# Letting the late weight blocks of a fused attention and two-MoE kernel into decoding in steps, tied to the stores of the second pass

## The chip, the cores and the metric

The kernel runs on one core of a Trainium2 chip. The metric is the device time of one execution in microseconds (us). The kernel before took 993.44 us (median of three executions, 986.15 to 995.56).

## The reference

Attention with a learned decay feeds a dense layer with a clipped gate, and that feeds a layer with the largest of three projections. Sizes: 4 batches, 8 heads, 576 positions, head width 64; 2304 tokens of width 512; inner widths 2048 and 768. The reference works in the precision of its weights, which come as 64-bit numbers.

```python
scores = q @ k.T / 8 + minimum(-(cum[:, None] - cum[None, :]), 0)   # causal, cum = cumsum(max(s, 0))
x  = softmax(scores) @ v                    # -> 2304 x 512
h  = x @ w_in                               # 512 x 2048
x2 = (h * clip(h + 3, 0, 6) / 6) @ w_out    # 2048 x 512
h2 = maximum(maximum(x2 @ w1, x2 @ w2), x2 @ w3)   # 512 x 768, three times
out = h2 @ w_out2                           # 768 x 512
```

## The kernel before

**A planner writes the order.** The kernel is written as coroutines ("threads"). A planner (class `Flow`, from L108) runs them against a small cost model of the engines (`mm`, `dve1`, `act2` and so on, from L196), and each time that it gives an engine to a thread, the thread emits the instruction. So the planner fixes, once and for all, the order of instructions on each engine and on the DMA queue (all DMAs are issued from SP, in `copy`, L306). On the chip each engine runs its list in that order, and waits only for the data and the buffers that an instruction really needs. A thread has a rank: of the threads ready for an engine, the lowest rank goes first. Buffers are held in stocks (`Stock`), and a thread that asks an empty stock waits by rank. A thread can also wait for an `Event`; such a wait exists in the plan only. A DMA's landing is planned by a formula (L184): 0.65 us, plus bytes over 360,000 per us, plus 0.9 us.

**Numbers as pairs.** Matrix products run in a reduced format; every operand is split into a high and a low part, and a product is three matmuls (L429 to L431, helper `three`), accumulated in one PSUM bank.

**Decoding a weight block** (`bits_in`, L373, and `decode`, L412). A block is 128 x 512 numbers of 64 bits, 512 KB. It is loaded into one of two `raw` buffers (stock RAW), squared on ACT (L385), and put together by four DVE instructions (L387, L393, L398, L403); the last frees the raw buffer. `decode` then rounds the block to its high part (L333, on DVE) and subtracts for the low part (L346, on POOL). For the third layer `raw_half` runs `bits_in` alone, straight into one half of a pair tile `wr`; two blocks make a pair, and there are nine pairs (NP2 = 9) for the eighteen blocks of w1, w2 and w3. `out_weight` decodes one of the six blocks of w_out2 (NJ = 6) and stores the result to DRAM (`o2_d`, shown as `o_d`), to be loaded again much later.

**Stages.** In the first (to some 372 us) attention runs, and in its gaps a first pass of the first layer: six of its sixteen inner blocks for all eight token blocks of 288 tokens (u = 0 to 7). Then follows the second pass with the other ten blocks. For each u, `hidden1` (L930) multiplies x by a block of w_in into a bank `ps_h`; `gate` (L951) makes `u` on ACT (L955), `g` on DVE (L959, which also frees the bank), and the pair `gt` (L331 on ACT, L346 on POOL or DVE). `reduce1` (L972) multiplies `gt` by a block of w_out into four banks `ps_x`. When a token block is complete, `x2_out` (L1025) adds, for each of the four banks, the first pass's part (`xf`, L1030 on DVE, which frees the bank), and stores the result to DRAM (`x2_d`, shown as `x_d<-xf`). When the four stores of u have landed, the event `x2_stored[u]` is set. TensorE's list alternates ps_h and ps_x matmuls all through this stage, with ps_h ahead by as many as nine `gt` tiles.

**The third layer** works on two token blocks at a time in seven products instead of eight. For this, `forms` (L1095) and `form` (L1110) make sums and differences of the pair tiles and split them (tiles `ws`, `wf`, `wg`). A form takes three or four buffers of the stock W2. These come from the second pass's weights, as its last token block gives them back, and three of them from `spare_weights` (L1078), which waits until all six blocks of w_out2 are stored. `hidden2` then multiplies (`ps_j`), and `reduce2` does the last product (`ps_o`).

**Ranks around the change.** NS = 160, NB = 10. Decoding of the second pass's weights has ranks 160 to 177, that of the pair blocks 180 to 197, that of w_out2 198 to 203. On engines other than TensorE, `gate` has rank 140 and `x2_out` has rank 200 (`RANKS`).

**Where the late decoding starts.** `main` (L1384) waits for the end of attention and then starts the threads of all forty-four blocks at once, at L1400 to L1409: ten of w_in, ten of w_out, nine pairs, six blocks of w_out2. As only two raw buffers exist, the blocks go through in order of rank.

Of the kernel before, what the change touches and what calls it, by code (L numbers as in the profile page):

```python
# [26 lines left out]
NJ = DF2 // P  # L27
# [227 lines left out]
def attn_moe_moe2(ctx, tc, q, k, v, s, w_in, w_out, w1, w2, w3, w_out2, out):  # L255
# [3 lines left out]
    flow = Flow()  # L259
    NB = NF - NA  # L260

    def event():
        return Event(flow)
# [28 lines left out]
    half = const.tile([P, 1], F32, name="half")  # L292
# [3 lines left out]
    def make(item, shape, dtype, name):  # L296
        pl, tag = item
        if pl is None:
            return views[tag]
        return pl.tile(shape, dtype, tag=tag, name=name, bufs=1)  # L300

    def stack(pl, tag, n):
        return [(pl, f"{tag}{x}") for x in range(n)]
# [66 lines left out]
    def weight(key):  # L370
        return ready.setdefault(key, event())

    def bits_in(src, out):  # L373
        r = yield RAW.get()
        raw = make(r, [P, 512], I64, "raw")
        yield DMA
        copy(raw, src)
        yield flow.landing(8 * P * 512)
        am = yield AM.get()
        m = make(am[1], [P, 512], F32, "dm")  # L380
        a = make(am[0], [P, 512], U32, "da") if out is None else out.bitcast(U32)
        bits = raw.bitcast(U32).rearrange("p (n t) -> p n t", t=2)
        lo, hi = bits[:, :, 0], bits[:, :, 1]
        yield "ACT", act1(512)
        act.activation(m, hi.bitcast(F32), AF.Square)  # L385
        yield "DVE", dve2(512)
        vec.scalar_tensor_tensor(  # L387
            out=m, in0=m, scalar=LEAST * LEAST, in1=hi.bitcast(F32),
            op0=ALU.is_ge, op1=ALU.mult,
        )  # L390
        top = m.bitcast(U32)
        yield "DVE", dve1(512)
        vec.tensor_scalar(  # L393
            out=a, in0=top, scalar1=3, scalar2=0x3FFFFFF8,
            op0=ALU.logical_shift_left, op1=ALU.bitwise_and,
        )
        yield "DVE", dve2(512)
        vec.scalar_tensor_tensor(  # L398
            out=a, in0=top, scalar=0xC0000000, in1=a,
            op0=ALU.bitwise_and, op1=ALU.bitwise_or,  # L400
        )
        yield "DVE", dve2(512)
        vec.scalar_tensor_tensor(  # L403
            out=a, in0=lo, scalar=29, in1=a,
            op0=ALU.logical_shift_right, op1=ALU.bitwise_or,
        )
        RAW.put(r)
        if out is not None:
            AM.put(am)
        return a.bitcast(F32), am  # L410

    def decode(src, store, key):  # L412
        item = yield store.get()
        wf, am = yield from bits_in(src, None)
        dst = make(item, [P, 2, 512], F32R, "w")
        yield from rounded(dst[:, 0, :], wf, 512, ON["wh"])
        yield from minus(dst[:, 1, :], wf, dst[:, 0, :].bitcast(F32), 512, ON["wl"])
        AM.put(am)
        weight(key).set((dst, item))
# [14 lines left out]
    NS = len(seq)  # L434
# [145 lines left out]
    def load(dst, src, nbytes):  # L580
        yield DMA
        copy(dst, src)
        return flow.landing(nbytes)
# [326 lines left out]
    x2_stored = [event() for u in range(NU)]  # L910
# [135 lines left out]
    NP2 = len(PAIRS)  # L1046
# [12 lines left out]
    def raw_pair(n):  # L1059
        item = yield W.get()  # L1060
        r = make(item, [P, 2, 512], F32, "wr")
        raw_item[n].set((r, item))

    def raw_half(n, half):
        r, _ = yield raw_item[n]
        i, j = PAIRS[n][half]
        yield from bits_in((w1, w2, w3)[i][j], r[:, half])
        raw_ready[n][half].set()

    def out_weight(j):  # L1070
        yield from decode(w_out2[j], W, ("o2", j))
        w, item = weight(("o2", j)).value
        ev = yield from load(o2_d[j], w, 8 * P * 512)
        yield ev
        W.put(item)
        o2_stored[j].set()

    def spare_weights():  # L1078
        for j in range(NJ):
            yield o2_stored[j]  # L1080
        for _ in range(2 * NA - NP2):
            W2.put((yield W.get()))
# [12 lines left out]
    def forms():  # L1095
        for n in range(NP2):
            for half in range(2):
                yield raw_ready[n][half]
            r, ri = raw_item[n].value
            items = []  # L1100
            for _ in range(3):
                items.append((yield W2.get()))
            made = [make(item, [P, 2, 2, HK], F32R, "wf") for item in items]
            if n % 2 == 0:
                spare = yield W2.get()
                single = make(spare, [P, 2, 2, HK], F32R, "wg")
            forms_of[n] = items + ([spare] if n % 2 else [])
            flow.start(flow.cur.prio, form(n, r, ri, made, single))
# [271 lines left out]
    def fill(stock_, items):  # L1380
        for item in items:
            stock_.put(item)

    def main():  # L1384
        yield attention_done
        pa.close()
        w2pool = ctx.enter_context(
            tc.tile_pool(name="w2pool", bufs=1, side="right", reuse_waits="tile")
        )
        psb = ctx.enter_context(  # L1390
            tc.tile_pool(name="psb", bufs=1, space=PSUM, side="right", reuse_waits="tile")
        )
        px2 = ctx.enter_context(
            tc.tile_pool(name="px2", bufs=1, side="right", reuse_waits="tile")
        )
        fill(M, stack(psb, "b", 5))
        fill(W2, stack(w2pool, "w", 2 * NB))
        for n in STAGE:
            fill(STAGE[n], [(px2, "xr" + n)])
        for f in range(NB):  # L1400
            flow.start(NS + f, decode(w_in[NA + f], W2, ("i", NA + f)))
        for f in range(NB):
            flow.start(NS + AFTER + f, decode(w_out[NA + f], W2, ("o", NA + f)))
        for n in range(NP2):
            flow.start(NS + 2 * NB + 2 * n, raw_pair(n))
            for half in range(2):
                flow.start(NS + 2 * NB + 2 * n + half, raw_half(n, half))
        for j in range(NJ):
            flow.start(NS + 2 * NB + 2 * NP2 + j, out_weight(j))  # L1409
        flow.start(0, spare_weights())  # L1410
        flow.start(NS, forms())
        yield part_stored[NU - 1]
        fill(XF, stack(mp, "part", 2))
        fill(PT, [(px2, "t0"), (px2, "t1")])
        yield x_over
        p_mx.close()
        mb1 = ctx.enter_context(
            tc.tile_pool(name="mb1", bufs=1, side="right", reuse_waits="tile")
        )
        fill(XFS, stack(mb1, "xf", 8))  # L1420
        for st in (UU, GG):
            XF.put((yield st.get()))
            PT.put((yield st.get()))

        def halved(item, *sts):
            t = make(item, [P, 2, U1], F32, "mm")
            for x, st in enumerate(sts):
                views[item[1], x] = t[:, x]
                st.put((None, (item[1], x)))

        for sts in ((MF, MF), (TMP, TMP), (MF, TMP)):
            halved((yield GT.get()), *sts)
        for _ in range(NG - 3):
            XFS.put((yield GT.get()))
        for j in range(NJ):
            yield o2_stored[j]
        yield mp_over
        for st in (MF, TMP, MF, MF):
            st.put((yield XF.get()))
            (MF if st is MF else TMP).put((yield PT.get()))  # L1440
        for _ in range(2):
            yield RAW.get()
            yield AM.get()
        p_dec.close()
        mb3 = p_out.enter_context(tc.tile_pool(name="mb3", bufs=1, reuse_waits="tile"))
        fill(AM, [((mb3, f"ws{x}"), None) for x in range(2)])
        fill(XFS, stack(mb3, "xf", 4))
        fill(W2, [(mb3, "w")])

    def late_weights():  # L1450
        yield heads[WO_AFTER].ready
        for f in range(NA):
            flow.start(WO_PRIO + WO_STEP * f, decode(w_out[f], W, ("o", f)))
# [15 lines left out]
    flow.start((NS + 2 + RANKS[3], -1), hidden2())  # L1469
    flow.start((NS + 1, -2), reduce2())  # L1470
    flow.start(0, main())
    flow.run()

# [55 lines left out]
```

## Time and profile before

| | |
|---|---|
| median of three executions | 993.44 us (986.15 to 995.56) |
| the profiled execution | 995.07 us |
| its span, first to last instruction | 993.3 us |
| mean granted TensorE clock, as a share of full speed | 0.958 |

The profile is of one execution. It gives each instruction's start and length, and for each idle time of an engine what ended it. A matmul's length overlaps its neighbours', so a stretch's number of matmuls tells its pace better than its busy time. The granted clock is TensorE's, 1.00 being 2.4 GHz; it has two levels, 2.4 and 1.2 GHz, and a share between them is a mean over a stretch.

### The profile page before, as it was taken

To read this page: it belongs to the slowest core of one execution; us is meant where nothing else is said; L and a number is where in the kernel's file an instruction comes from. 1 tells how busy PE (TensorE), PEld (TensorE's weight loads), DVE (VectorE), ACT (ScalarE), POOL (GpSimd) and SP (SyncE) were. 2 spreads that over 40 slices of the span, in tenths; PEclk is the share of its full clock that TensorE was granted. 3 is DMA by queue.
4 is the path that set the end of the run, shared out by engine and by line. 5 is a ranking of instruction groups with operands and counts; after the bars stand their busy time and mean duration, and the time that the engine had idled before them with its cause. 6 is when DMAs were issued, how large, how long until landed. Compare 5 with 4: busy or idle time off the path is not lost.

```text
span 993.3 us, 19077 instructions
## 1 busy us (share of the span) xinstructions
PE 938.8 (95%) x6532; PEld 876.1 (88%) x6532; DVE 693.2 (70%) x1818; ACT 452.4 (46%) x1146; POOL 389.0 (39%) x431
## 2 busy tenths in 40 slices
PE   9998799899899999899899999999799999999998
PEld 5454589889788999799899999999799999999998
DVE  5887889789888728999888842239977676666300
ACT  3566578677676744343443333335433232333311
POOL 4668757656555423444234332225740101021000
PEclk7779799999998999999999999999899999999999
DMA  5789877686684435555676743201203030264522
GB/s 170 188 206 239 234 181 209 174 242 172 171 225 109 144 109 192 177 185 172 182 219 203 249 144 96 85 12 48 84 31 91 25 96 25 67 206 137 162 84 73
DMA packets 87482, 144.56 MB, mean 146 GB/s; under 512 B 9532, under 2 KB 58684, under 8 KB 87384
## 3 DMA queue, kind: packets, MB, share of 16 engines
q1 hardware_dynamic: 87384, 143.33, 49.8%
q8 instruction: 52, 0.85, 0.4%
q14 instruction: 46, 0.38, 0.1%
HBM read 82.79 MB, written 33.96 MB: 118 GB/s over the span
## 4 chain that ended last, share of the span: by engine, by line
PE 60%; DVE 15%; DMA 13%; issue 5%; ACT 3%; SPq 2%; POOL 1%; DVEq 0%; ACTq 0%; POOLq 0%
PE ps_j L430 7%; PE ps_j L431 6%; PE ps_j L429 6%; PE ps_s L762 5%; DMA kt<-kb 5%; PE ps_h L429 3%; PE ps_h L430 3%; PE ps_h L431 3%; PE pt L826 3%; PE ps_x L429 3%; PE ps_x L431 3%; PE ps_x L430 3%; PE px L867 3%; DMA raw<-in_w_dram 3%; PE ps_o L430 3%
## 5 line engine op out<-in xcount | busy, mean ns | idle before, releaser
L429 PE MATMUL ps_x<-gt,w 128*128 128x288 f32 x512 | 155.1, 303 | 7.1 <-DVE g L959 6.7
L346 POOL TENSOR_TENSOR gt<-g,gt 128x288 fp32r<-128x288 f32 x101 | 88.1, 872 | 186.0 <-ACT gt L331 174.4
L429 PE MATMUL ps_h<-x,w 128*128 128x288 f32 x512 | 154.4, 301 | 2.7 <-DVE g L959 1.7
L431 PE MATMUL ps_x<-gt,w 128*128 128x288 f32 x512 | 152.8, 298 | 1.5 <-POOL w L346 1.5
L430 PE MATMUL ps_h<-x,w 128*128 128x288 f32 x512 | 152.0, 297 | 0.0
L430 PE MATMUL ps_x<-gt,w 128*128 128x288 f32 x512 | 151.9, 297 | 0.0
L431 PE MATMUL ps_h<-x,w 128*128 128x288 f32 x512 | 151.7, 296 | 0.0
L340 POOL TENSOR_SCALAR e<-e,tiny 128x256 f32<-128x256 f32 (+4 forms) x152 | 104.8, 696 | 93.8 <-DVE tiny L791 44.4
L430 PE MATMUL ps_j<-xf,wf 128*128 128x288 f32 x432 | 130.0, 301 | 3.1 <-POOL xf L346 2.7
L429 PE MATMUL ps_j<-xf,wf 128*128 128x288 f32 x432 | 129.5, 300 | 2.1 <-DVE xf L333 2.0
L431 PE MATMUL ps_j<-xf,wf 128*128 128x288 f32 x432 | 129.5, 300 | 0.0
L762 PE MATMUL ps_s<-kt,qt 66*128 66x256 f32 (+11 forms) x384 | 102.9, 364 | 14.1 <-DMA kt<-kb 10.4
L785 ACT ACTIVATE e<-e,tiny 64x576 f32<-64x576 f32 (+4 forms) x160 | 95.8, 599 | 38.6 <-DVE tiny L777 33.0
L331 ACT ACTIVATE gt<-g 128x288 fp32r<-128x288 f32 x128 | 56.5, 443 | 119.1 <-DVE g L959 118.9
L959 DVE SCALAR_TENSOR_TENSOR g<-u,ps_h 128x288 f32<-128x288 f32 x128 | 57.1, 446 | 71.6 <-ACT u L955 71.3
L429 PEld LDWEIGHTS ps_x<-gt,w 128*128 128x128 f32 x512 | 97.8, 191 | 9.9 <-DVE g L959 8.1
L429 PEld LDWEIGHTS ps_h<-x,w 128*128 128x128 f32 x512 | 97.1, 190 | 4.1 <-DVE g L959 2.2
L431 PEld LDWEIGHTS ps_x<-gt,w 128*128 128x128 f32 x512 | 97.7, 191 | 1.9 <-POOL w L346 1.9
L430 PEld LDWEIGHTS ps_x<-gt,w 128*128 128x128 f32 x512 | 98.0, 191 | 0.0
L430 PEld LDWEIGHTS ps_h<-x,w 128*128 128x128 f32 x512 | 97.2, 190 | 0.1
L431 PEld LDWEIGHTS ps_h<-x,w 128*128 128x128 f32 x512 | 97.1, 190 | 0.0
L777 DVE CUSTOM_DVE_ANT_0 e<-ps_s,above 64x288 f32<-64x288 f32 (+4 forms) x160 | 75.3, 474 | 30.4 <-PE ps_s L762 29.1
(149 smaller groups left out, 2234.9 us busy)
## 6 DMA issues: line engine op xcount, KB each, us to landing
x<-x_d SPq DMA_DIRECT2D x64, 288.0 KB
kt<-kb SPq DMA_DIRECT2D x90, 144.0 KB
raw<-in_w_out_dram SPq DMA_DIRECT2D x22, 512.0 KB
x_d<-xs SPq DMA_DIRECT2D x16, 576.0 KB
raw<-in_w_dram SPq DMA_DIRECT2D x18, 512.0 KB
qt<-qb SPq DMA_DIRECT2D x30, 288.0 KB
raw<-in_w_in_dram SPq DMA_DIRECT2D x16, 512.0 KB
mh<-m_d SPq DMA_DIRECT2D x48, 144.0 KB
```

Source lines behind the costliest of these rows:

```text
L331: act.activation(dst, src, AF.Copy)
L340: (pool if e == "POOL" else vec).tensor_scalar(out=y, in0=y, scalar1=r, scalar2=1.0, op0=ALU.mult, op1=ALU.mult)
L346: (pool if e == "POOL" else vec).tensor_tensor(out=dst, in0=a, in1=b_, op=ALU.subtract)
L429: pe.matmul(ps, lhsT=wh, rhs=xh, start=first, stop=False, skip_group_check=again)
L430: pe.matmul(ps, lhsT=wh, rhs=xl, start=False, stop=False, skip_group_check=again)
L431: pe.matmul(ps, lhsT=wl, rhs=xh, start=False, stop=last, skip_group_check=again)
L762: pe.matmul(o, lhsT=lhs[:, qs], rhs=rhs[:, lo:hi], start=(x == 0), stop=(x == len(passes) - 1),)
L777: vec.tensor_tensor_reduce(out=e[:n, lo:hi], in0=ps[:n, 0:hi - lo], in1=above[:n, shift + lo:shift + hi], scale=-0.125, scalar=m0, op0=ALU ...
L785: act.activation(e[:n, :w], e[:n, :w], AF.Exp, bias=m0, scale=-1.0, accum_out=r,)
L826: pe.transpose(pt[:, y, :], cut, ident[:n, :n])
L867: pe.matmul(px[:, z:n], lhsT=vhl[:, x, j].rearrange("p l d -> p (l d)"), rhs=src[:, hl, x, z:n], start=(x + hl == 0), stop=(last and hl == 1),
L959: vec.scalar_tensor_tensor(out=g, in0=ut, scalar=1.0, in1=ps, op0=ALU.min, op1=ALU.mult)
```

## The change

The loops that start the pair blocks and the blocks of w_out2 leave `main`. A new thread, `later_weights`, starts them in steps. Pairs 0 and 1 are started when `x2_stored[0]` is set, pairs 2 and 3 at `x2_stored[1]`, 4 and 5 at `x2_stored[2]`, 6 and 7 at `x2_stored[3]`, and pair 8 at `x2_stored[4]`. With pairs 3 to 8 goes one block of w_out2 each. So the five steps hold 4, 5, 6, 6 and 3 blocks. The ranks stay as they were.

```diff
@@ -1401,12 +1401,7 @@
             flow.start(NS + f, decode(w_in[NA + f], W2, ("i", NA + f)))
         for f in range(NB):
             flow.start(NS + AFTER + f, decode(w_out[NA + f], W2, ("o", NA + f)))
-        for n in range(NP2):
-            flow.start(NS + 2 * NB + 2 * n, raw_pair(n))
-            for half in range(2):
-                flow.start(NS + 2 * NB + 2 * n + half, raw_half(n, half))
-        for j in range(NJ):
-            flow.start(NS + 2 * NB + 2 * NP2 + j, out_weight(j))
+        flow.start(0, later_weights())
         flow.start(0, spare_weights())
         flow.start(NS, forms())
         yield part_stored[NU - 1]
@@ -1446,6 +1441,16 @@
         fill(AM, [((mb3, f"ws{x}"), None) for x in range(2)])
         fill(XFS, stack(mb3, "xf", 4))
         fill(W2, [(mb3, "w")])
+
+    def later_weights():
+        for n in range(NP2):
+            if n % 2 == 0:
+                yield x2_stored[n // 2]
+            flow.start(NS + 2 * NB + 2 * n, raw_pair(n))
+            for half in range(2):
+                flow.start(NS + 2 * NB + 2 * n + half, raw_half(n, half))
+            if n > 2:
+                flow.start(NS + 2 * NB + 2 * NP2 + n - 3, out_weight(n - 3))
 
     def late_weights():
         yield heads[WO_AFTER].ready
```

## Rows read from the trace of the kernel before

**Rows 1.** The page's first part: busy time, share of the span, instructions.

```profile
PE 938.8 (95%) x6532; PEld 876.1 (88%) x6532; DVE 693.2 (70%) x1818; ACT 452.4 (46%) x1146; POOL 389.0 (39%) x431
```

**Rows 2.** By stretch: PE, PEld, DVE, ACT, POOL busy; granted clock, DMA share, GB/s.

```profile
372.00:465.00 93.00, 87.79 (x647) 86.86 (x646) 87.92 (x127) 37.31 (x82) 41.29 (x33) 0.98 0.57 177
...
472.00:484.00 12.00, 9.28 (x52) 8.18 (x51) 10.47 (x21) 4.75 (x10) 2.70 (x3) 0.86 0.59 190
484.00:544.00 60.00, 60.00 (x456) 60.00 (x455) 48.77 (x82) 24.80 (x50) 20.88 (x20) 1.00 0.68 210
544.00:552.00 8.00, 6.83 (x48) 6.16 (x48) 5.97 (x12) 2.64 (x6) 2.65 (x3) 1.00 0.69 208
...
576.00:584.00 8.00, 7.27 (x52) 6.66 (x51) 5.05 (x11) 1.67 (x4) 2.86 (x3) 1.00 0.58 201
584.00:640.00 56.00, 56.00 (x426) 56.00 (x425) 11.28 (x25) 17.28 (x37) 15.33 (x19) 1.00 0.25 75
...
675.00:735.00 60.00, 52.81 (x354) 51.45 (x354) 56.90 (x108) 26.48 (x69) 40.09 (x43) 0.91 0.19 56
```

**Rows 3.** TensorE's waits from 465 to 500 us: total, times, longest.

```profile
PE ps_x L431 <- POOL w L346: 1.5, 2, 0.9
PE ps_x L429 <- DVE g L959: 1.2, 1, 1.2
```

**Rows 4.** Timeline of TensorE, 475 to 484 us.

```profile
476.90 0.40 PE L429 MATMUL ps_x<-gt,w 128*128 128x288 f32 x1 [1.21 <-DVE g L959]
...
480.13 0.40 PE L429 MATMUL ps_h<-x,w 128*128 128x288 f32 x1 [1.14 <-DVE g L959]
...
481.25 0.44 PE L430 MATMUL ps_x<-gt,w 128*128 128x288 f32 x1
...
483.64 0.44 PE L431 MATMUL ps_h<-x,w 128*128 128x288 f32 x1
```

**Rows 5.** Timeline of DVE, 470 to 477 us.

```profile
470.43 1.62 DVE L387 SCALAR_TENSOR_TENSOR dm<-dm,raw 128x512 f32<-128x512 f32 x1
...
474.13 0.45 DVE L959 SCALAR_TENSOR_TENSOR g<-u,ps_h 128x288 f32<-128x288 f32 x1
475.65 0.83 DVE L387 SCALAR_TENSOR_TENSOR dm<-dm,raw 128x512 f32<-128x512 f32 x1 [1.07 <-ACT dm L385]
476.41 0.44 DVE L959 SCALAR_TENSOR_TENSOR g<-u,ps_h 128x288 f32<-128x288 f32 x1
```

**Rows 6.** Timeline of the DMA queue on SP, 465 to 614 us.

```profile
465.35 0.33 SPq L306 DMA_DIRECT2D raw<-in_w_dram  x1
...
478.31 0.33 SPq L306 DMA_DIRECT2D x_d<-xf  x1
...
484.76 0.32 SPq L306 DMA_DIRECT2D x_d<-xf  x1
...
570.04 0.34 SPq L306 DMA_DIRECT2D raw<-in_w_out_dram  x1
...
612.70 0.32 SPq L306 DMA_DIRECT2D x_d<-xf  x1
```

**Rows 7.** DVE's groups by line, 465 to 582 us: busy, mean ns, idle before.

```profile
L387 DVE SCALAR_TENSOR_TENSOR dm<-dm,raw 128x512 f32<-128x512 f32 x25 | 18.8, 752 | 13.7 <-ACT dm L385 13.6
...
L403 DVE SCALAR_TENSOR_TENSOR wr<-raw,wr 128x512 uint32<-128x512 uint32 x18 | 15.1, 841 | 0.2
L398 DVE SCALAR_TENSOR_TENSOR wr<-dm,wr 128x512 uint32<-128x512 uint32 x18 | 13.3, 736 | 0.5
L393 DVE TENSOR_SCALAR wr<-dm 128x512 uint32<-128x512 uint32 x18 | 10.2, 569 | 0.2
...
L333 DVE CAST w<-da 128x512 fp32r<-128x512 f32 x8 | 3.8, 472 | 0.1
```

**Rows 8.** DVE's groups by line, 584 to 640 us.

```profile
L959 DVE SCALAR_TENSOR_TENSOR g<-u,ps_h 128x288 f32<-128x288 f32 x19 | 8.6, 454 | 40.2 <-ACT u L955 40.2
```

**Rows 9.** Timeline of DVE: the first instruction of the first form.

```profile
660.71 0.42 DVE L1090 TENSOR_TENSOR ws<-wr 128x256 f32<-128x256 f32 x1
```

## The prediction

> **What bounds the kernel now.** Start with the page's first part: TensorE is busy for 95% of the span, VectorE (DVE) for 70% [rows 1]. So no edit off TensorE can give more than TensorE loses now, and the question is where it loses. Next comes the table by stretch, read by matmul counts, since lengths overlap. In 484 to 544 us TensorE starts 456 matmuls in 60 us, one each 0.1316 us, at a granted clock of 1.00; 584 to 640 has the same pace (426 in 56) [rows 2]. That is the full pace of this stage. Against it:
>
> - 472 to 484: 52 matmuls are worth 6.84 us, so 5.16 us of 12 are lost.
> - 544 to 552: 48 are worth 6.32 us, 1.68 lost.
> - 576 to 584: 52 are worth 6.84 us, 1.16 lost.
> - 675 to 735: 354 are worth 46.6 us, 13.4 lost, with DVE busy for 56.90 of 60 us. This is the forms' stretch, and the changed threads don't run there [all rows 2].
>
> The first three lie where a token block of the second pass ends: its stores stand in the DMA queue from 478.31 to 484.76 for u = 0, and each later token block comes some 32 us after ((612.70 - 484.76) / 4 for u = 0 to 4) [rows 6]. The pair blocks enter the queue at 465.35, and the last block of w_out2 at 570.04 [rows 6], so the changed threads' work lies over all three losses. Then the waits: around the largest one TensorE waits for `g` on DVE, and, before that, for the last block of w_out on POOL (1.5 us) [rows 3]. The timeline shows how: TensorE stands at 476.90 and 480.13 for `g` [rows 4]. On DVE, a decode instruction from 470.43 takes 1.62 us, others follow up to the `g` of 474.13, and the next `g` comes at 476.41, behind a decode instruction that itself sat 1.07 us until ACT had squared a block [rows 5]. DVE works through its list in order, so a `g` that is ready stands behind a decode instruction that isn't.
>
> **The change, part by part.** *What is removed and added:* nothing. The same 24 blocks are loaded, squared, put together and stored. No wait is added on the chip either: the waits for `x2_stored` exist in the plan, and what changes is where the 24 loads, 24 squarings, the DVE work and six stores stand in the lists of SP, ACT, DVE and POOL. The first load behind a store needs only a free raw buffer.
>
> *Size of what is moved.* From the first load to the last, 23 intervals take 104.7 us, 4.55 us a block [rows 6]. On DVE a block costs 0.75 + 0.57 + 0.74 + 0.84 = 2.90 us, with 0.47 more for the rounding of w_out2 [rows 7]; idle before the first of these, for ACT, was 13.6 us over 25 blocks, 0.54 us each [rows 7].
>
> *Where it goes.* The five steps hold 4, 5, 6, 6 and 3 blocks and begin after the stores of u = 0 to 4. I add 2 us for the landing as the planner counts it (0.65 + 0.41 + 0.9). They then last 18.2, 22.8, 27.3, 27.3 and 13.7 us. From the last store of one token block to the first store of the next there are 32 - (484.76 - 478.31) = 25.5 us [rows 6]. So step 0 ends 5 us ahead of the next boundary; step 1 (24.8 us) just reaches it; steps 2 and 3 (29.3 us) run over it; step 4 ends at 612.7 + 15.7 = 628.4, where no boundary is near.
>
> *Boundary of u = 0 (472 to 484).* It loses all its decode work. What stays there on DVE is `g`, `xf` and some `gt`; a boundary without decode work, that of u = 4 inside 584 to 640, loses nothing [rows 2]. The ends are 0 (the wait is owed to the backlog of the earlier decoding, where DVE was busy for 87.92 of 93 us [rows 2]) and -5.2 us. I take -5.2, since the rows on DVE name the decode instructions.
>
> Of the 5.2 us some belong to a slow clock: from 481.25 to 483.64 eleven matmuls start 0.239 us apart [rows 4], nearly twice 0.1316, so the clock was at 1.2 GHz, after the waits of TensorE just told; the stretch's mean is 0.86 [rows 2].
>
> The Trainium skill, "TensorE: Matmul & The Clock Gate", section on HAM oscillation, says that gaps in TensorE's work drop it back to half rate, so that a wait is paid a second time behind it. By this rule, with which the trace agrees here (0.239 us after the waits), the slow stretch goes with the waits, and the sum stands; were it to come anyway, 13 matmuls from 480.84 on by 0.107 us, 1.4 us of the gain would stay lost.
>
> *Boundary of u = 1 (510 to 518).* No loss now, with decode work beside it (inside 484 to 544 [rows 2]), none after: 0.
>
> *Boundary of u = 2 (544 to 552).* Step 1 may or may not be over. Ends 0 and -1.7 us; I take half, -0.8.
>
> *Boundary of u = 3 (576 to 584).* Step 2 lies over it as w_out2 does now. Ends -1.2 and +0.5 (it loses what u = 2 loses now); I take 0.
>
> *Boundary of u = 4 (608 to 613).* Now free; step 3 will lie over it. Ends 0 and +5.2 (what u = 0 loses now); I take +1.4, the mean of the losses now at u = 2 and u = 3, as these are the boundaries whose DVE lists look alike.
>
> *Inside the token blocks.* TensorE loses nothing from 484 to 544 with DVE busy for 48.77 of 60 us [rows 2]. Between 584 and 640 DVE has 11.28 us of work in 56 [rows 2], a `g` every 3 us or so and 40.2 us idle beside them [rows 8]. Steps 3 and 4 bring nine blocks, some 28 us there. That is covered: 0. If that cover were missing, it would show as at u = 4.
>
> *The late end.* The first form starts at 660.71 [rows 9]. `spare_weights` now ends at about 630 (628.4 and a store) instead of some 585, so 30 us of slack hide the delay.
>
> *Sum.* -5.2 + 0 - 0.8 + 0 + 1.4 + 0 = -4.6 us, from -8.1 (the low ends) to +5.7 (the high ends). The profiled execution took 995.07 us, 1.6 above the median of 993.44. 995.07 - 4.6 = 990.5 for such an execution; by the median, **988.8 us**.
>
> **Rivals.**
>
> *A, the stall doesn't come from the decoding.* DVE comes out of 372 to 465 with a backlog (95% busy) and TensorE first waits for the last w_out block on POOL [rows 2, 3]; `g` would be late in any case. Against it: the instructions ahead of the late `g` are decode instructions of the moved blocks [rows 5]. Gain 0: 993.4 us.
>
> *B, the stall moves with the decoding (the slower side).* A step starts as a burst, two loads at once with an empty ring, and ends about when the next token block does. `x2_out` has rank 200 and the decoding 180 to 203, so at a boundary the plan lets decode instructions go ahead of nearly every `xf`, and banks stay taken. Place: boundaries of u = 2, 3 and 4. Price: each pays what u = 0 pays now, so -5.2 + (5.2 - 1.7) + (5.2 - 1.2) + 5.2 = +7.5: 1000.9 us. It decides from the point where a block takes more than 25.5 / 6 = 4.2 us in steps 2 and 3, and where TensorE has no `gt` in stock. For it: 4.55 us a block. Against: u = 2 and 3 have such work now and pay 1.7 and 1.2.
>
> *C, the whole loss goes.* With pauses between the steps DVE catches up, and all three boundaries run at full pace: -5.2 - 1.7 - 1.2 = -8.1: 985.4 us. For it: at u = 1 decode work costs nothing now. Against: steps 2 and 3 leave no pause.
>
> *D, the forms wait.* If the last block of w_out2 is stored after 660.71 instead of near 630, W2 lacks three buffers and each us past it is lost; ten late would give 1003 us. Against: 30 us of slack [rows 6, 9].
>
> *E, the change does not do what it says.* If TensorE and its feeders run behind the plan, loads planned after a store may run beside the next boundary all the same; by its result that is A (993.4 us) or B (1000.9 us), and its chance is counted in theirs.
>
> **How the numbers follow.** The forecast gets 0.48, A 0.20, C 0.15, B 0.12, D 0.05. The forecast's own range goes from 985 (C's end) to 993 (A's end). The three executions of before lie 9.4 us apart, so medians move by some 4 us on their own. Downward I go 5 us below C, to 980; upward to 1000, which takes in A whole and about half of B. Left out are half of B, D, and a small tail of C: under 2 in 10. About 1%, 9.9 us, is what a measurement of this kernel can tell from no change. Faster by more than that (under 983.5) needs C with a good draw, or the forecast with a very good one: 0.15 x 0.4 + 0.48 x 0.15 = 0.13, and 0.01 from A: 0.14. Slower by more (over 1003.4): D's 0.05 halved and a third of B: 0.07. The rest, 0.79, is within 1%.
>
> **What would show it.** Right: no raw load in the queue between the last block of w_out and the last store of u = 0; some 90 matmuls in the 12 us around that boundary at a granted clock of 1.00; a raw load shortly behind each of the stores of u = 0 to 4; the last store of w_out2 near 625; DVE busy for 35 to 45 us from 584 to 640, instead of 11.28, with TensorE still at 0.1316 us a matmul; the first form within a few us of 655. Wrong: waits for `g` at the first boundary without decode work ahead of them (A); new waits for `g` or `xf` near 608, 579 or 545 with a granted clock below 1.00 behind them (B); a first form held by its buffers (D). A shift of more than some us within the forms' stretch would lie outside all of these.

## The result, and the profile after

The changed kernel is faster: 981.71 us (median of thirteen executions, 978.68 to 985.40) against 991.38 us (thirteen executions, 986.15 to 995.56). The ratio is 0.9917, with a 95% interval from 0.9899 to 0.9936, so 8.2 us are gained, between 6.3 and 10.0 (the medians alone lie 9.7 us apart). The forecast was 4.6 us, to 988.8 us.

The profiled execution of the changed kernel took 978.72 us, with a span of 976.9 us. Its span is 16.4 us shorter than that of the kernel before [the page's head], twice what the timing shows, and so the first thing to do is to split this difference. The lists of TensorE, DVE, ACT and POOL are the same in both kernels up to the last block of w_out; TensorE's is the same to its end. The subtraction for the low part of that block (`w<-da,w` on POOL, the last one ahead of the stores of u = 0) is a mark that both traces have. In the timeline of POOL of the kernel before (start, length, engine, line):

```profile
470.23 1.28 POOL L346 TENSOR_TENSOR w<-da,w 128x512 fp32r<-128x512 f32 x1 [1.82 <-DVE w L333]
```

and of the changed kernel:

```profile
462.00 1.28 POOL L346 TENSOR_TENSOR w<-da,w 128x512 fp32r<-128x512 f32 x1 [1.82 <-DVE w L333]
```

The changed kernel's execution is 8.23 us ahead there, before the first instruction on DVE, ACT or POOL that the change moved. In the kernel before the first late load is in the queue by then (465.35 [rows 6]), but it has no part in this: matched matmul by matmul, TensorE is 8.2 us ahead already at 350 us, in the attention stage. That half is the difference between two executions of the same lists, not the change. From the end of attention on executions of the same lists agree better: from the matmul that the kernel before starts at 372 us to the mark, the nine traces with the same lists there took between 98.2 and 98.9 us. From here on every time is counted from this mark.

In the DMA queue of the changed kernel:

```profile
470.25 0.32 SPq L306 DMA_DIRECT2D x_d<-xf  x1
...
471.14 11.31 SPq L306 DMA_DIRECT2D raw<-in_w_dram  x4
...
613.16 0.33 SPq L306 DMA_DIRECT2D o_d<-w  x1
...
629.89 0.32 SPq L306 DMA_DIRECT2D x_d<-xf  x1
...
696.57 0.33 SPq L306 DMA_DIRECT2D x_d<-xf  x1
```

and two later stores in that of the kernel before:

```profile
644.69 0.32 SPq L306 DMA_DIRECT2D x_d<-xf  x1
...
711.22 0.33 SPq L306 DMA_DIRECT2D x_d<-xf  x1
```

The reader is to see two things. The late loads now stand behind the last store of u = 0 (470.25, then 471.14), where before they stood ahead of the first [rows 6], and the last store of w_out2 comes at 613. And the gain can be followed along the marks:

| from the mark to | before | changed | difference |
|---|---|---|---|
| last store of u = 0 | 14.53 us | 8.25 us | -6.3 us |
| last store of u = 5 | 174.46 us | 167.89 us | -6.6 us |
| last store of u = 7 | 240.99 us | 234.57 us | -6.4 us |
| end of the span | 523.1 us | 514.9 us | -8.2 us |

Most of the gain is there after the first boundary. A last 1.8 us come in the forms' stretch and behind. The stores between these marks say less, as a store also shifts with the DVE work around it (last store of u = 4: 142.5 and 139.7 us). TensorE's 6532 matmuls, matched one by one, split the 8.2 us behind the mark better: 5.4 us are gained at the boundary of u = 0, 1.3 at that of u = 2, nothing in the end at u = 3, 0.3 are lost at u = 4, and 1.7 are gained in the forms' stretch. The table by stretch of the changed kernel (columns as in [rows 2]); the first row lies to the mark as 472 to 484 did, the next three run from the last store of one token block to that of the next (u = 2, 3 and 4), the last is the forms' stretch, moved by the 14.7 us that it starts earlier:

```profile
463.77:475.77 12.00, 12.00 (x93) 12.00 (x92) 4.02 (x10) 5.14 (x12) 4.03 (x5) 1.00 0.60 185
500.67:535.74 35.07, 34.77 (x263) 34.51 (x262) 24.38 (x39) 11.98 (x25) 13.30 (x12) 1.00 0.60 195
535.74:569.40 33.66, 32.72 (x246) 32.25 (x245) 25.62 (x43) 13.21 (x28) 12.52 (x12) 1.00 0.61 197
569.40:601.73 32.33, 32.33 (x245) 32.09 (x244) 23.41 (x41) 12.60 (x26) 9.41 (x10) 1.00 0.64 200
...
660.30:720.30 60.00, 53.51 (x371) 52.15 (x370) 57.76 (x106) 26.88 (x70) 40.63 (x44) 0.94 0.19 56
```

TensorE has 93 matmuls where it had 52 (the view counts those that reach over an edge), at a granted clock of 1.00 instead of 0.86, and DVE is busy for 4.02 us instead of 10.47. At 0.1316 us a matmul 41 more are 5.4 us. At u = 2 now 35.07 - 263 x 0.1316 = 0.46 us are lost (1.68 before), at u = 3 1.29 (1.16 before), at u = 4 0.09 (none before). In DVE's timeline the boundary of u = 0 looks like this:

```profile
463.52 0.44 DVE L959 SCALAR_TENSOR_TENSOR g<-u,ps_h 128x288 f32<-128x288 f32 x1
464.86 0.45 DVE L959 SCALAR_TENSOR_TENSOR g<-u,ps_h 128x288 f32<-128x288 f32 x1 [0.90 <-ACT u L955]
465.23 0.81 DVE L1030 TENSOR_TENSOR xf<-ps_x,pt 128x288 f32<-128x288 f32 x2
...
475.85 0.69 DVE L387 SCALAR_TENSOR_TENSOR dm<-dm,raw 128x512 f32<-128x512 f32 x1 [0.25 <-ACT dm L385]
```

Each `g` and `xf` starts as its data comes, and the first decode instruction of the late blocks comes more than 13 us behind the mark; before, it came 0.2 us behind it [rows 5].

### The profile page after: what moved, and what is told of

It is laid out like the page before. It is cut to its first block, busy times and chain, and to the rows that moved or that the text cites. A ratio compares the mean times of both kernels' runs of the same rounds, so it can differ in the third digit from the quotient of the medians.

```text
span 976.9 us, 19063 instructions
## 1 busy us (share of the span) xinstructions
PE 931.7 (95%) x6532; PEld 870.5 (89%) x6532; DVE 701.5 (72%) x1819; ACT 451.7 (46%) x1146; POOL 390.0 (40%) x430
## 4 chain that ended last, share of the span: by engine, by line
PE 66%; DVE 14%; DMA 9%; issue 5%; POOL 2%; ACT 2%; SPq 2%; DVEq 0%; POOLq 0%; ACTq 0%
PE ps_j L430 6%; PE ps_j L431 6%; PE ps_j L429 6%; PE ps_s L762 6%; PE ps_x L429 4%; PE ps_h L429 4%; PE ps_h L430 4%; PE ps_x L431 4%; PE ps_h L431 4%; PE ps_x L430 4%; PE pt L826 3%; DMA kt<-kb 3%; PE px L867 3%; PE ps_o L430 3%; PE ps_o L431 3%
## 5 line engine op out<-in xcount | busy, mean ns | idle before, releaser
L955 ACT ACTIVATE u<-ps_h,half 128x288 f32<-128x288 f32 x128 | 63.5, 496 | 61.2 <-PE ps_h L431 60.6
```

Of the source, the lines that this page charges most:

```text
L955: act.activation(ut, ps, AF.Relu, bias=half, scale=1.0 / 6.0)
```

## The experiments

TensorE's own list is the same in the kernel before, the changed kernel and all experiments but the last two: only the lists of DVE, ACT, POOL and SP differ. The ratios come from three sets, each against the kernel before on one chip: the first four experiments; the two with landings 2 us later together with the two that only move the rounding; the remaining four. A ratio of one set is compared with that of another, or with the changed kernel's 0.9917, across sets. At the end of this section one table has those with the same list.

**All late blocks together, behind the stores of u = 0.** The pauses go, the free boundary stays.

```diff
     def later_weights():
         for n in range(NP2):
-            if n % 2 == 0:
-                yield x2_stored[n // 2]
+            if n == 0:
+                yield x2_stored[0]
```

> All 24 late blocks start together when the stores of token block u = 0 have landed; no steps after that. Theory T (the loss sits at the boundary of u = 0, where DVE comes out of the backlog of the w_out decoding, and only the absence of decode work there counts): the gain stays nearly whole, 6 to 8 us, ratio 0.992 to 0.994 to the kernel before; TensorE starts some 90 matmuls in the 12 us around the boundary of u = 0. Theory P (the pauses between the steps are what counts): at most 3 us, 0.997 or more, with new losses at u = 1 to u = 3.

Measured: 0.9944 (0.9919 to 0.9968), 5.5 us. The 12 us at the boundary of u = 0, in the table by stretch:

```profile
463.64:475.64 12.00, 12.00 (x93) 12.00 (x92) 4.02 (x10) 5.03 (x11) 4.04 (x5) 1.00 0.60 184
```

93 matmuls, as in the changed kernel. So theory T holds, a hair above its range: one free boundary is worth most of the gain. Whether the four further steps add the remaining 2.7 us can't be said, as the intervals of 0.9917 and 0.9944 overlap.

**The first step at once, the others as changed.**

```diff
-            if n % 2 == 0:
+            if n % 2 == 0 and n > 0:
                 yield x2_stored[n // 2]
```

> Pairs 0 and 1 start at the end of attention as before, so they follow the last w_out block at once; pairs 2 to 8 and w_out2 keep the steps of the changed kernel. Theory T: four blocks last some 18 us and cover the boundary of u = 0 as before, so the loss of 5 to 6 us there comes back; ratio 0.998 to 1.000. Theory P: most of the gain stays, ratio 0.993 to 0.995.

Measured: 0.9987 (0.9961 to 1.0012). The same 12 us, and TensorE's waits in them (total, times, longest):

```profile
462.71:474.71 12.00, 9.27 (x54) 8.44 (x53) 10.80 (x22) 4.86 (x10) 2.82 (x4) 0.86 0.58 189
```

```profile
PE ps_x L429 <- DVE g L959: 1.2, 1, 1.2
PE ps_h L429 <- DVE g L959: 1.1, 1, 1.1
```

54 matmuls, a clock of 0.86 and the waits for `g` of [rows 4]: the loss is back. With the experiment above this is the change taken apart: that the late blocks wait for the stores of u = 0 carries it, and the other steps alone give at most 0.4%.

**The second pass's sums ahead of decoding.** Kernel before; only the rank of `x2_out` changes.

```diff
-flow.start(flow.cur.prio, (part_out if z == 0 else x2_out)(u, d, *banks[d], count))
+flow.start((MOE, 150) if z else flow.cur.prio, (part_out if z == 0 else x2_out)(u, d, *banks[d], count))
```

> The kernel before, but the sums and stores of the second pass (x2_out) get rank 150 in place of 200 off TensorE, so the plan puts them ahead of decoding; the blocks start where they did. Theory R (the plan's order of xf behind decode instructions keeps the PSUM banks taken): 4 to 6 us faster, ratio 0.994 to 0.996. Theory T (it is g that stands behind decode instructions, and g already had the better rank): 0 to 1.5 us, ratio 0.9985 to 1.000, with TensorE still waiting for g at the boundary of u = 0.

Measured: 1.0004 (0.9985 to 1.0023). This rank does not do it, as theory T had it, and TensorE still waits for `g` (1.5 us in 469 to 500). At the boundary 65 matmuls run in place of 52, but the loss comes back behind it: the last store of u = 5 stands 176.4 us from the mark, where it was 174.5.

**The steps two token blocks later.**

```diff
-                yield x2_stored[n // 2]
+                yield x2_stored[n // 2 + 2]
```

> The five steps of the changed kernel tied to the stores of u = 2 to 6 in place of 0 to 4, 64 us later. All theories: the boundary of u = 0 is free (some 6 us gained). The late end then decides (D of the prediction): the last six to nine blocks, 3 us of DVE work each, fall into the forms' stretch, where DVE is full. If the slack is used up: 5 to 20 us slower than the changed kernel, ratio 0.997 to 1.012. If the forms don't need these blocks early: the changed kernel's own 0.992.

Measured: 1.0157 (1.0122 to 1.0191), 15.5 us slower, and worse than the range expected. The boundary of u = 0 is free here too (93 matmuls), and the last store of u = 5 stands at 169.5 us, so the price falls behind it. The table by stretch and TensorE's waits:

```profile
706.00:736.00 30.00, 14.44 (x68) 13.97 (x68) 28.32 (x48) 9.14 (x22) 14.56 (x14) 0.60 0.25 83
```

```profile
PE ps_j L429 <- ACT mm L1233: 14.2, 1, 14.2
```

68 matmuls where 228 fit at full pace. The wait of 14.2 us is for a copy on ACT, and ACT's timeline shows why the copy was late:

```profile
723.12 0.68 ACT L385 ACTIVATE dm<-raw 128x512 f32<-128x512 f32 x1 [2.52 <-DVE wr L398]
727.28 0.67 ACT L385 ACTIVATE dm<-raw 128x512 f32<-128x512 f32 x1 [3.48 <-DMA raw<-in_w_dram]
727.85 0.99 ACT L1233 ACTIVATE mm<-ps_j 128x288 f32<-128x288 f32 x3
```

The three copies stand behind the squarings of late blocks, and the last of these waits 3.48 us for its load. The 160 missing matmuls are worth 21 us; two thirds of that is this wait, and the granted clock of 0.60 adds to it. This is the late end of the prediction's rival D, but not at the place that it named: the wait that the trace shows is that of the forms' products, behind late decode work in ACT's list. The first form stands 206.1 us from the mark, 184.1 in the changed kernel; whether the plan held it back for buffers the trace doesn't show, as such a wait exists in the plan only.

**Later landings in the plan.** The four above say where the loss sits, not why. There are two ways for decode work to hold TensorE up: DVE has too much to do there (W), or decode instructions stand in the list before their data has come, and what is ready waits behind them (H). The planner counts 2.0 us from the issue of a 512 KB load to its landing (0.65 + 0.41 + 0.9). The chain of the kernel before that ended last has them longer:

```profile
479.27 3.66 DMA raw<-in_w_dram
...
487.08 3.56 DMA raw<-in_w_dram
...
494.77 3.50 DMA raw<-in_w_dram
...
502.59 4.77 DMA raw<-in_w_dram
```

So the plan is given 2 us more for the 24 late blocks, in the kernel before and in the changed one. The threads start as before, and the first late load is still issued at once behind those of w_out (4.9 us ahead of the mark in both). As the plan now holds a raw buffer longer, the later loads spread: the last is issued 109.6 us behind the mark, 99.8 before.

```diff
-    def bits_in(src, out):
+    def bits_in(src, out, late=0.0):
...
-        yield flow.landing(8 * P * 512)
+        ev = flow.landing(8 * P * 512); ev.time += late; yield ev
...
-        yield from bits_in((w1, w2, w3)[i][j], r[:, half])
+        yield from bits_in((w1, w2, w3)[i][j], r[:, half], 2.0)
...
-        yield from decode(w_out2[j], W, ("o2", j))
+        yield from decode(w_out2[j], W, ("o2", j), 2.0)
```

> The kernel before, but the plan counts each load of the 24 late blocks as landing 2 us later than its formula, so that their squarings and DVE instructions stand further back in the lists, behind work that is ready. Starts stay as before. Theory H (the loss at u = 0 comes from decode instructions that stand in DVE's list before their data is there): 3 to 6 us faster than the kernel before, ratio 0.994 to 0.997. Theory W (it comes from the amount of DVE work that the late blocks put beside the end of the w_out backlog): 0 to 1.5 us, ratio 0.9985 to 1.0.

> The changed kernel with the same later landings in the plan for the 24 late blocks. Theory H: up to 2 us better than the changed kernel (0.9917), ratio 0.989 to 0.992, since what is left at u = 2 and 3 goes. Theory W: the changed kernel's own ratio, 0.990 to 0.993.

Measured: 0.9886 (0.9827 to 0.9945) for the kernel before, 0.9876 (0.9812 to 0.9940) for the changed one. The kernel before gets the whole gain, 11.3 us (5.4 to 17.1), though its late blocks still start at the end of attention. That is theory H's direction, but more than the 3 to 6 us that it was given. The 12 us at the boundary of u = 0 and DVE's timeline in it:

```profile
462.04:474.04 12.00, 11.08 (x80) 10.43 (x79) 11.02 (x20) 4.58 (x10) 3.95 (x4) 1.00 0.58 185
```

```profile
462.38 0.44 DVE L959 SCALAR_TENSOR_TENSOR g<-u,ps_h 128x288 f32<-128x288 f32 x1
...
465.02 0.44 DVE L959 SCALAR_TENSOR_TENSOR g<-u,ps_h 128x288 f32<-128x288 f32 x1
465.38 0.44 DVE L1030 TENSOR_TENSOR xf<-ps_x,pt 128x288 f32<-128x288 f32 x1
466.59 0.84 DVE L387 SCALAR_TENSOR_TENSOR dm<-dm,raw 128x512 f32<-128x512 f32 x1 [0.77 <-ACT dm L385]
```

DVE is even busier than in the kernel before (11.02 of 12 us against 10.47 [rows 2]), and yet TensorE has 80 matmuls instead of 52 at a clock of 1.00. So it is not the amount of DVE work in these 12 us, and W falls. The `g` and `xf` now stand ahead of a decode instruction that waits. In the changed kernel, later landings add too little to be told from it (0.9876 against 0.9917, overlapping intervals), though its trace has the shortest way from the mark to the last store of u = 5, 165.6 us.

**The same knob both ways.** The kernel before, with 1 us less and 1 us more (the two 2.0 above become -1.0 and 1.0).

> The kernel before, with the 24 late blocks' loads planned as landing 1 us sooner than the formula. Theory H (decode instructions stand in DVE's list ahead of their data): the loss around u = 0 to u = 3 grows, 2 to 6 us slower than the kernel before, ratio 1.002 to 1.006. Theory W (the amount of work): 0.999 to 1.001. Rival N (any other order than that of before helps, since before had an unlucky one): below 0.997.

> The kernel before, with the same loads planned as landing 1 us later, half the step that gave 0.9886. Theory H: between the two, 0.990 to 0.996. Theory W: 0.9985 to 1.0.

Measured: 1.0091 (1.0062 to 1.0119) for 1 us sooner, 0.9894 (0.9862 to 0.9926) for 1 us later. Both go the way of theory H and further than its ranges, at +1 only just; +1 and +2 can't be told apart by their ratios. From the mark to the last store of u = 5 it is 184.7 us at -1, 174.5 at 0, 169.7 at +1 and 167.1 at +2: the loss follows the knob in both directions. The amount of decode work does not follow it: the DVE instructions L387 to L403 of the late blocks take 71.4, 70.3, 74.5 and 71.4 us at -1, 0, +1 and +2, and from the first late load to the last it is 107.5, 104.7, 110.6 and 114.5 us. At -1 TensorE waits for (470 to 592 us):

```profile
PE ps_x L429 <- DVE g L959: 8.8, 3, 4.4
PE ps_x L429 <- DVE xf L1030: 2.4, 2, 1.7
```

The longest of these, 4.4 us, ends with a `g` that DVE reaches 5.9 us after the one before it, behind decode instructions of which two waited for their squarings:

```profile
547.40 0.44 DVE L959 SCALAR_TENSOR_TENSOR g<-u,ps_h 128x288 f32<-128x288 f32 x1
548.35 0.69 DVE L387 SCALAR_TENSOR_TENSOR dm<-dm,raw 128x512 f32<-128x512 f32 x1 [0.50 <-ACT dm L385]
...
552.04 0.69 DVE L387 SCALAR_TENSOR_TENSOR dm<-dm,raw 128x512 f32<-128x512 f32 x1 [1.33 <-ACT dm L385]
...
553.25 0.45 DVE L959 SCALAR_TENSOR_TENSOR g<-u,ps_h 128x288 f32<-128x288 f32 x1
```

So N falls as well: it is not that any other order would do. How much of the loss is DVE standing idle ahead of a decode instruction, and how much is a `g` or `xf` behind decode instructions that are ready, isn't split: DVE's idle time before L387, from 5 us ahead of the mark to 122 us behind it, is 15.4, 13.7, 5.6 and 9.4 us for -1, 0, +1 and +2, so at +2 it is more than at +1 while the loss is less. At +1 the boundary of u = 0 still has only 62 matmuls, and most of its gain comes at the later ones.

**Less DVE work ahead of the boundary.** The rounding of the second pass's 20 blocks goes to ACT, in the kernel before and in the changed one.

```diff
-    def decode(src, store, key):
+    def decode(src, store, key, wh=ON["wh"]):
...
-        yield from rounded(dst[:, 0, :], wf, 512, ON["wh"])
+        yield from rounded(dst[:, 0, :], wf, 512, wh)
...
-decode(w_in[NA + f], W2, ("i", NA + f))
+decode(w_in[NA + f], W2, ("i", NA + f), ACT)
-decode(w_out[NA + f], W2, ("o", NA + f))
+decode(w_out[NA + f], W2, ("o", NA + f), ACT)
```

> The kernel before, with the rounding to the high part of the second pass's 20 weight blocks on ACT in place of DVE (20 DVE instructions of 0.43 to 1.1 us less before the boundary of u = 0). Backlog theory (the late blocks cost so much at u = 0 because DVE comes out of the 20 blocks late): the stretch of the 20 blocks gets shorter and the boundary of u = 0 loses less than 3 us in place of 6; ratio 0.985 to 0.993. If the late blocks alone make the loss: the boundary still loses 5 us or more, ratio 0.993 to 0.998.

> The changed kernel with the same rounding on ACT. Backlog theory: the gains overlap, so this is 0.982 to 0.988, less than the sum of the two. If they are independent: the product of 0.9917 and the ratio of the kernel before with rounding on ACT. If the DVE list of the 20 blocks is not what holds TensorE there: 0.9917.

Measured: 0.9974 (0.9939 to 1.0010) and 0.9899 (0.9867 to 0.9930). In the kernel before the boundary has 76 matmuls, a loss of 2.0 us, as the backlog theory had it, but the time moves less than that theory's range and can't be told from none, and the stretch of the 20 blocks gets no shorter (98.0 us from the matmul at 372 us to the mark, 98.2 before). The changed kernel with it can't be told from the one without. The backlog helps to set what the boundary costs, though the order of DVE's list shifts with it, and the two aren't parted here. DVE's rounding isn't what the 20 blocks' stretch hangs on.

**Later landings for all 44 blocks**, alone and with the rounding on ACT (the changed kernel with 2.0 given to the starts of w_in and w_out too). Here TensorE's list changes.

> The changed kernel, with the loads of all 44 blocks (the second pass's 20 too) planned 2 us later. TensorE's own order changes here. Theory H: the waits for g between the end of attention and the last w_out block (5.2 us in the kernel before) go in part, 2 to 5 us beyond 0.9876: 0.982 to 0.987. If DVE's amount of work holds TensorE there: 0.986 to 0.990.

> The same, with the rounding of the second pass's 20 weight blocks on ACT as well. If DVE's amount of work is the limit in the stretch of the 20 blocks: 2 to 4 us better than the one without, 0.979 to 0.985. If not: the same as the one without.

Measured: 0.9935 (0.9909 to 0.9962) and 0.9899 (0.9869 to 0.9929). The first is a miss. TensorE's waits in 370 to 475 us:

```profile
PE ps_x L431 <- POOL w L346: 3.5, 5, 0.8
PE ps_x L429 <- DVE w L333: 3.2, 3, 2.0
```

The waits for `g` (5.2 us before in this stretch) are gone, and 6.7 us of waits for the weights stand in their place: there the blocks are wanted at once, and what is put back in DVE's list arrives later. A further gain by this knob needs blocks that have time. With the rounding on ACT it comes back to the changed kernel's level, between what the two theories expected.

Side by side (12 us: at the boundary of u = 0, placed to the mark like 472 to 484; us: from the mark to the last store of u = 5, and to the end of the span):

| kernel | matmuls in 12 us | to u = 5 | to the end | ratio |
|---|---|---|---|---|
| before | 52 | 174.5 | 523.1 | 1 |
| changed | 93 | 167.9 | 514.9 | 0.9917 |
| all at the first store | 93 | 168.4 | 515.5 | 0.9944 |
| first step at once | 54 | 172.0 | 519.4 | 0.9987 |
| sums ahead | 65 | 176.4 | 523.9 | 1.0004 |
| two steps later | 93 | 169.5 | 536.7 | 1.0157 |
| before, landings +2 | 80 | 167.1 | 514.4 | 0.9886 |
| changed, landings +2 | 93 | 165.6 | 513.5 | 0.9876 |
| before, landings -1 | 59 | 184.7 | 532.6 | 1.0091 |
| before, landings +1 | 62 | 169.7 | 516.8 | 0.9894 |
| before, rounding on ACT | 76 | 172.7 | 520.7 | 0.9974 |
| changed, rounding on ACT | 93 | 167.8 | 515.0 | 0.9899 |

No experiment beats the changed kernel by more than the intervals allow.

## Why the prediction was right

The direction, the place and the mechanism were right; the size was short, 4.6 us for a measured 8.2 (6.3 to 10.0). Of the signs that it named, these came: 93 matmuls at a clock of 1.00, a raw load shortly behind each of the five stores, DVE busy for 38.75 of the 56 us that match 584 to 640, and the last store of w_out2 151.2 us from the mark, where 625 stood for 154.8.

- *Boundary of u = 0, -5.2 us:* right. TensorE's matmuls there are worth 5.4 us more, and the slow clock went with the waits (granted clock 0.86 before, 1.00 after). This agrees with the Trainium skill, "TensorE: Matmul & The Clock Gate", section on HAM oscillation, by which gaps in TensorE's work bring the half rate. The gaps that this section reckons with are longer than any of the waits here, the longest of which is 1.21 us [rows 4]; on that the measurement decides. That the decode instructions of the late blocks are the cause, rival A's question, was settled by starting only the first step as before: 54 matmuls, 0.9987. A falls.
- *That a ready `g` stands behind a decode instruction that isn't ready:* right for the wait that ends at 476.90, ahead of which DVE stood 1.07 us [rows 5]. From that stop to the wait that ends at 480.13 DVE was busy throughout, so there the `g` stood behind decode instructions that were ready as well. Together they are more of the whole than I had made it. I priced the boundaries as if work beside them cost by its amount. The runs with the plan's landings moved show that the place in the list decides most of it.
- *Boundary of u = 2, -0.8:* it gave -1.2. *u = 3, 0:* +0.1.
- *Boundary of u = 4, +1.4:* the step of the sum that was mis-sized. It lost 0.1 us up to its last store, 0.3 us in all by the matched matmuls. Step 3 does lie over it, as reckoned, and I took the mean loss of two other boundaries as its price; u = 1, which had decode work beside it and lost nothing, was the nearer row. Rival B falls with it: its burst is there, its price isn't.
- *Inside the token blocks, 0:* right.
- *The forms' stretch, 0:* the second mis-sized step. It came out 1.8 us shorter from the last store of u = 7 on, with the lists of DVE, ACT and POOL the same there. 371 matmuls start in its 60 us instead of 354, at a granted clock of 0.94 instead of 0.91. Whether the change has a part in this stays open: the profiled executions of the experiments with the same work there lie between 280.2 and 282.4 us from that store to the end, so it may be chance. Without it the traces give the change 6.4 us.
- *The late end hidden:* right for the steps as they are (the first form starts 184.1 us from the mark, 190.5 before), and the slack is real but not endless: two token blocks later cost 24 us against the changed kernel (1.0157 against 0.9917).
- *Rival C, 985.4 us:* nearest by its number, but by luck, and not by its mechanism: u = 3 still loses 1.3 us, and without the pauses that it rests on u = 5 comes as soon (168.4 us from the mark, 167.9 with them).

The boundaries add up to -5.4 - 1.2 + 0.1 + 0.1 = -6.4 us, against -6.6 by the marks and -6.4 by the matched matmuls.

## What to carry to other kernels

Where engines run fixed lists, ask of each instruction not only what it costs but whether its data is there when its turn comes; an instruction that is put ahead of its load's landing holds up what stands behind it, and an engine's busy share doesn't show it: DVE was busy for 10.47 of 12 us where TensorE lost most, and for 11.02 where it lost much less. So compare the latency that a plan assumes with the one that the trace has before moving work about: here 2 us in a formula did as much as moving 24 blocks, as far as the intervals tell. And align two traces at the last instruction that both have in common before a difference is put down to a change.

## What was not expected of the hardware

Two executions of the same lists were 8.2 us apart by the end of the w_out decoding (470.23 and 462.00), as much as the whole effect of the change. And the granted clock fell to half after waits of which none was longer than 1.21 us [rows 4]. It did so at that boundary in the kernel before, with the first step at once, and with landings 1 us sooner and 1 us later (0.86 over the 12 us); in the other runs of the table it stood at 1.00.

One thing the prediction's reading passed over: the decode instruction of 1.62 us at 470.43 [rows 5] ran beside POOL's 1.28 us of the mark. Of the 96 late decode instructions on DVE in that trace (L387 to L403), the 49 that ran while POOL was idle took at most 0.70 us each, the 47 beside POOL 0.88 us on average. No run here tests what this adds to the loss.
